# Twelve elementwise steps of a gated-recurrence and maxout kernel moved to GpSimd, with every engine's order kept

## The chip, the cores and the metric

One core of a Trainium2 chip runs the whole program. The metric is the device time of one execution in microseconds, the median of several runs. The engines are named as in the profile: PE (TensorE, the matrix unit), DVE (VectorE), ACT (ScalarE), POOL (GpSimd) and SP (SyncE, which issues most loads and stores). Each engine works through its own instructions in order; an instruction that waits for another engine or for a DMA holds up everything behind it on its own engine.

## What is computed

A gated linear recurrence over 4 batches, 8 heads, 768 steps and head size 48, with complex gates a, and then a feed-forward part whose hidden layer is the maximum of three products:

```python
mag = np.sqrt(a_re * a_re + a_im * a_im)
scale = np.minimum(mag, 0.999) / (mag + 1e-06)
a_re_n, a_im_n = (a_re * scale, a_im * scale)
...
for t in range(S):
    ar, ai = (a_re_n[:, :, t, :, None], a_im_n[:, :, t, :, None])
    new_re = ar * S_re - ai * S_im
    new_im = ar * S_im + ai * S_re
    kv = np.einsum('bhd,bhe->bhde', k[:, :, t], v[:, :, t])
    S_re, S_im = (new_re + kv, new_im)
    y[:, :, t] = np.einsum('bhd,bhde->bhe', q[:, :, t], S_re)
...
h = np.maximum(np.maximum(x @ w1, x @ w2), x @ w3)
return (h @ w_out).astype(np.float32)
```

x is y with the heads side by side: 3072 tokens of 384; w1, w2, w3 are 384 x 768, w_out is 768 x 384.

## The kernel before

**Tiling.** The tokens are cut into 12 groups (0 to 11) of two tiles, x and y, of 128 tokens each. For every group the program takes the gates to logarithm and angle (`gates`, `angles`), forms decay factors by matmuls with fixed 0/1 tables and exponentials, turns and scales k and q, transposes them, computes scores, states and outputs (`y`), and then the feed-forward part: `up` (three products and their maximum) and `op` (the product with w_out, for later groups by a seven-product scheme). The matmuls of group 0's feed-forward part begin while the weights are still being prepared.

**Order.** What runs when is written out by hand: SCHEDULE is a list of words, each `name:group`. `run` turns a word into instructions and the class `Bound` ties every instruction to the one before it on its engine, so each engine follows the list's order exactly. SLOTS hands out the banks of PSUM, and OTHER is a set of words that take the second of two engines where a step can run on either (VectorE for most).

**Weights.** They come in twelve blocks of 128 x 768 elements (0 to 11). For block i, `WLi` loads the raw words, `Wai` changes the type of their upper halves into a scratch (`ex`, the lower or the upper part of the tile `xhx`), and `Wei` (VectorE) merges the scratch with the lower halves into the weight tile. Blocks 0, 6, 10, 1, 4, 7 use the lower scratch, the others the upper one, so a `Wa` has to wait for the `We` before it on the same scratch. `Wgi` adds block i - i % 3 to block i, by an accumulating DMA that POOL issues, or on VectorE. `T`, `t` and `M` transpose blocks of w1 and multiply them with w_out; `Mn` reads the copies in vb2, vb3 and uk2, which `Z2`, `Z3` and `Z4` clear on POOL after that.

**Gates.** `sqr` and `sqi` square the two parts (tiles e and L), `add` sums them, `lnL` takes the logarithm, `expe` and `lne` make the correction of the 1e-06, `relu` writes the limited logarithm into the tile Ln, and `Lnop` adds the correction to it by an accumulating DMA from POOL. `abs`, `lnw`, `atan`, `turn` and others make the angle. `Cd` is a carry of a few numbers from one group to the next, two small DMAs from POOL for each tile, which `turn` of the next group waits for. `half` and `xor` work on sign bits.

**POOL before.** Besides those DMAs it makes the constant tables at the start, clears tiles, and in `CL` (`constants_late`) makes the late masks with the tile KB as scratch and clears the two score tiles atm0 and atm1.

Of the kernel before, what the change touches and what calls it, by code (L numbers as in the profile page):

```python
# [16 lines left out]
I32 = mybir.dt.int32  # L17
# [124 lines left out]
Px:10 P2:10 P6:10 P7:10  # L142
""".split())

ROOMS = {0: "w1", 3: "w2", 6: "wo", 11: "w1", 1: "w2", 9: "H", 10: "S", 2: "H", 4: "S", 5: "H", 7: "S", 8: "H"}
EX = (0, 6, 10, 1, 4, 7)

# [2 lines left out]
def kernel(  # L150
# [103 lines left out]

    def magnitude(out, in_):

        if other():
            dve.tensor_single_scalar(out=out.bitcast(I32), in_=in_.bitcast(I32), scalar=0x7FFFFFFF, op=OP.bitwise_and)
        else:
            activation(out=out, in_=in_, func=AF.Abs)  # L260
# [189 lines left out]
    def weight_step(i, step):  # L450

        dst, src = blocks[i]
        n, m = dst.shape[1:]
        ex = xhx[:, 0:KD] if i in EX else xhx[:, KD + KF:]
        ex = ex.rearrange("p f t -> p (f t)").rearrange("p (n m) -> p n m", n=n)
        if step == "a":
            high = T["raw", i].bitcast(BF).rearrange("p n (m w) -> p n m w", w=4)[:, :, :, 2]
            out = ex.bitcast(F16).rearrange("p n (m w) -> p n m w", w=2)[:, :, :, 1]
            if other():
                dve.tensor_single_scalar(out=out, in_=high, scalar=-1.0 if i in (0, 3, 6) else 1.0, op=OP.mult)  # L460
            else:
                activation(out=out, in_=high, func=AF.Copy, scale=-1.0 if i in (0, 3, 6) else 1.0)
        elif step == "e":
            low = T["raw", i].bitcast(I32).rearrange("p n (m w) -> p n m w", w=2)[:, :, :, 0]
            dve.scalar_tensor_tensor(out=dst.bitcast(I32), in0=low, scalar=13, in1=ex.bitcast(I32),
                                     op0=OP.logical_shift_right, op1=OP.bitwise_or)
        else:
            increase(dst, blocks[i - i % 3][0])
# [47 lines left out]
    def gates(g, cs, name):  # L516
# [19 lines left out]

        L, w, e, ar, ai = (part(nm) if (nm, g) in T else None for nm in ("L", "w", "e", "ar", "ai"))
        if name == "sqr":
            activation(out=e, in_=ar, func=AF.Square)
        elif name == "sqi":  # L540
            activation(out=L, in_=ai, func=AF.Square)
        elif name == "add":
# [5 lines left out]
        elif name == "expe":  # L548
            activation(out=e, in_=L, func=AF.Exp, scale=-0.5)
        elif name == "lne":  # L550
            if g >= ADDS and "relu:%d" % g not in OTHER:
                activation(out=e, in_=e, func=AF.Ln, scale=1e-6 * math.exp(-LNMAX), bias=math.exp(-LNMAX))
            else:
                activation(out=e, in_=e, func=AF.Ln, scale=1e-6, bias=1.0)
        elif name == "relu":
            T["Ln", g] = lns[g % 2]
            if other():
                dve.tensor_scalar(out=part("Ln"), in0=L, scalar1=-0.5, scalar2=-LNMAX, op0=OP.mult, op1=OP.max)
            else:
                activation(out=part("Ln") if g >= ADDS else L, in_=L, func=AF.Relu, scale=-0.5, bias=LNMAX)  # L560
# [26 lines left out]
        elif name == "xor":  # L587
            dve.scalar_tensor_tensor(out=ai.bitcast(I32), in0=ar.bitcast(I32), scalar=-0x80000000, in1=ai.bitcast(I32),
                                     op0=OP.bitwise_and, op1=OP.bitwise_xor)
        elif name == "half":  # L590
            dve.tensor_scalar(out=ar.bitcast(I32), in0=ar.bitcast(I32), scalar1=31, scalar2=HALF,
                              op0=OP.arith_shift_right, op1=OP.bitwise_and)
        elif name == "atan":
            activation(out=w, in_=w, func=AF.Arctan)
        elif name == "turn":
            dve.scalar_tensor_tensor(out=w, in0=w, scalar=-1.0 / math.pi, in1=ar, op0=OP.mult, op1=OP.add)
# [476 lines left out]
```

## Time and profile before

| | |
|---|---|
| three runs | 545.36, 543.21, 546.37 us; median 545.36 |
| the profiled execution | 543.15 us, its span 541.4 us |
| busy of the span | PE 95%, DVE 88%, ACT 68%, POOL 12% |
| granted TensorE clock | 1.00 |

A span is the time from the first instruction to the last. Times in the rows below are microseconds from its start. In a row of a timeline the first number is the start, the second the duration, then engine, line and operation, the tile written and the tiles read (buffer numbers left out), the form and the count; in square brackets the engine's idle time before it and what ended that. L210 is the line of the helper through which every instruction is recorded, so instructions are told apart by their tiles. A row of a group gives busy time and the mean of one in ns. Busy time of an engine says little by itself: what a step is worth depends on which engine ends last in its stage.

### The profile page before, as it was taken

What the parts mean: (1) busy time and instruction counts of PE and PEld (TensorE: products, weight loads), DVE (VectorE), ACT (ScalarE), POOL (GpSimd) and SP (SyncE); (2) the same over time, 40 slices, a digit from 0 to 9 for tenths busy, and PEclk for the clock granted to TensorE, in tenths of its full rate; (3) what the DMA queues carried; (4) which work ended last, traced back from release to release, by engine and by line L of the source; (5) the groups of instructions that cost most, each with busy time, mean ns of one, the idle gap of its engine ahead of it and who ended that gap; (6) DMA issues with size and microseconds to landing.
All of it is one profiled execution on the core that took longest, in us unless ns stands there. A gap on an engine that the chain in (4) does not pass through costs nothing.

```text
span 541.4 us, 24280 instructions
## 1 busy us (share of the span) xinstructions
PE 512.1 (95%) x10918; PEld 438.9 (81%) x10918; DVE 477.2 (88%) x746; ACT 367.9 (68%) x646; POOL 63.4 (12%) x107
## 2 busy tenths in 40 slices
PE   1499899999999999999999999999999999999996
PEld 1266778788988888888788888979888887988996
DVE  5999999999999999999789899899899979979414
ACT  7999887976874987667687576686779545451100
POOL 8424200110200110001200200020030020000000
PEclk9999999999999999999999999999999999999999
DMA  8999845553514045146226314035064042000001
GB/s 206 297 235 213 200 82 86 92 108 72 108 30 78 18 92 101 34 85 115 40 45 125 51 37 90 8 58 115 9 114 80 5 68 55 19 19 2 4 0 59
DMA packets 140152, 44.08 MB, mean 81 GB/s; under 512 B 130320, under 2 KB 138128, under 8 KB 140048
## 3 DMA queue, kind: packets, MB, share of 16 engines
q1 hardware_dynamic: 136272, 37.76, 32.9%
q0 software_dynamic: 3776, 4.76, 5.2%
q8 instruction: 86, 1.41, 1.1%
q14 instruction: 18, 0.15, 0.1%
HBM read 33.02 MB, written 4.72 MB: 70 GB/s over the span
## 4 chain that ended last, share of the span: by engine, by line
PE 86%; ACT 8%; DVE 2%; issue 2%; POOL 2%; DVEq 0%; ACTq 0%; POOLq 0%
PE up L210 35%; PE op L210 23%; PE y L210 7%; PE A L210 5%; PE tp L210 4%; PE dk L210 4%; PE sums L210 3%; PE cs L210 2%; PE F L210 2%; PE B L210 1%; ACT L L210 1%; ACT xhx L210 1%; ACT e L210 1%; ACT L210 1%; POOL cuts L210 1%
## 5 line engine op out<-in xcount | busy, mean ns | idle before, releaser
L210 PE MATMUL up<-xhx,w 128*128 128x256 f32 (+1 forms) x1062 | 177.7, 381 | 0.0
L210 PEld LDWEIGHTS up<-xhx,w 128*128 128x128 f32 (+1 forms) x1062 | 144.4, 163 | 24.8 <-issue 0.6
L210 ACT ACT_TABLE_LOAD x47 | 60.3, 1283 | 1.6 <-PEq L1057 0.8
L210 POOL DMA_DIRECT2D ar<-nf x40 | 33.3, 1226 | 153.8 <-DVE ar L210 102.5
L210 PE MATMUL op<-wo,xhx 128*128 128x192 f32 (+3 forms) x358 | 49.6, 368 | 0.0
L210 DVE TENSOR_TENSOR Q<-Q,f 112x512 f32<-112x512 f32 (+1 forms) x48 | 44.9, 953 | 0.0
L210 ACT COPY atm<-B 32x128 f32<-32x128 f32 x96 | 24.6, 256 | 28.9 <-PE B L210 16.7
L210 PE MATMUL y<-atm,vb 128*32 128x64 f32 x1152 | 39.8, 220 | 3.3 <-issue 3.3
L210 PE MATMUL y<-QG,g 112*32 112x64 f32 x1408 | 39.2, 219 | 1.4 <-issue 1.4
L210 PEld LDWEIGHTS op<-wo,xhx 128*32 128x32 f32 (+1 forms) x358 | 35.6, 149 | 4.3 <-issue 1.2
L210 PEld LDWEIGHTS y<-QG,g 112*32 112x32 f32 x1408 | 35.4, 109 | 4.1 <-issue 4.0
L210 PEld LDWEIGHTS y<-atm,vb 128*32 128x32 f32 x1152 | 34.7, 109 | 4.3 <-issue 2.5
L210 ACT ACTIVATE f<-F 48x232 f32<-48x232 f32 x96 | 34.2, 359 | 4.9 <-PE F L210 3.6
L210 DVE TENSOR_TENSOR xhx<-xhx,up 128x768 f32<-128x768 f32 x22 | 20.8, 951 | 18.2 <-PE up L210 18.1
L210 ACT ACTIVATE xhx<-up 128x768 f32<-128x768 f32 x17 | 13.8, 812 | 31.4 <-PE up L210 30.2
L210 PE MATMUL op<-wo,strassen 128*128 128x192 f32 (+1 forms) x272 | 33.0, 328 | 0.0
L210 PEld LDWEIGHTS A<-Q,K 112*32 112x32 f32 x1536 | 28.6, 110 | 5.0 <-issue 2.7
L210 DVE COPY_PREDICATED atm<-masko,A 128x256 f32<-128x256 uint8 x72 | 31.3, 438 | 1.4
L210 PE MATMUL A<-Q,K 112*32 112x80 f32 x1536 | 32.0, 233 | 0.7 <-issue 0.5
L210 PE MATMUL op<-w,strassen 128*128 128x192 f32 (+1 forms) x296 | 32.4, 328 | 0.0
L210 DVE TENSOR_TENSOR QG<-Q,f 112x1024 f32<-112x1024 f32 (+1 forms) x24 | 27.1, 1131 | 4.7 <-PE y L210 4.0
L210 PE MATMUL cs<-w,upto 128*32 128x192 f32 (+1 forms) x320 | 21.4, 344 | 9.4 <-POOL KB L210 6.7
(146 smaller groups left out, 1061.1 us busy)
## 6 DMA issues: line engine op xcount, KB each, us to landing
ai<-in_a_im_dram SPq DMA_DIRECT2D x24, 192.0 KB, 4.1
ar<-in_a_re_dram SPq DMA_DIRECT2D x24, 192.0 KB, 4.3
q<-in_q_dram SPq DMA_DIRECT2D x96, 48.0 KB, 2.9
k<-in_k_dram SPq DMA_DIRECT2D x96, 48.0 KB, 2.9
vb<-in_v_dram SPq DMA_DIRECT2D x96, 48.0 KB, 2.8
out_dram<-ot SPq DMA_DIRECT2D x23, 192.0 KB, 3.4
Ln<-e POOLq DMA_DIRECT2D x7, 384.0 KB, 4.9
w<-in_moe_w_dram SPq DMA_DIRECT2D x3, 767.2 KB, 7.9
```

The lines of the kernel that those rows point to most:

```text
L210: ins = f(*a, **kw)
```

## The change

A set POOLED of twelve words is added. Words in it run on POOL: the type changes Wa0, Wa6 and Wa11 (on VectorE before) and Wa3, Wa10, Wa9 and Wa1 (on ScalarE before); the limits relu:1 (VectorE) and relu:2, relu:4 (ScalarE); the squares sqr:2 and sqr:5 (ScalarE, by its Square function; on POOL a product of the tile with itself). A limit made on ScalarE leaves a constant factor that `lne` of its group takes out; for the moved ones `lne` uses the other form, as it did for limits on VectorE. The branches for `abs` and `half` are added too, but no word of theirs is in the set. SCHEDULE, SLOTS, OTHER and all else stay.

```diff
+POOLED = set("""
+Wa0:0 Wa6:0 Wa3:0 Wa10:0 Wa9:0 Wa1:0 Wa11:0 relu:1 relu:2 relu:4 sqr:2 sqr:5
+""".split())
...
     def magnitude(out, in_):
 
-        if other():
+        if T["word"] in POOLED:
+            pool.tensor_single_scalar(out=out.bitcast(I32), in_=in_.bitcast(I32), scalar=0x7FFFFFFF, op=OP.bitwise_and)
+        elif other():
...
-            if other():
+            if T["word"] in POOLED:
+                pool.tensor_single_scalar(out=out, in_=high, scalar=-1.0 if i in (0, 3, 6) else 1.0, op=OP.mult)
+            elif other():
                 dve.tensor_single_scalar(out=out, in_=high, scalar=-1.0 if i in (0, 3, 6) else 1.0, op=OP.mult)
...
         if name == "sqr":
-            activation(out=e, in_=ar, func=AF.Square)
+            if T["word"] in POOLED:
+                pool.tensor_tensor(out=e, in0=ar, in1=ar, op=OP.mult)
+            else:
+                activation(out=e, in_=ar, func=AF.Square)
...
-            if g >= ADDS and "relu:%d" % g not in OTHER:
+            if g >= ADDS and "relu:%d" % g not in OTHER | POOLED:
...
-            if other():
+            if T["word"] in POOLED:
+                pool.tensor_scalar(out=part("Ln"), in0=L, scalar1=-0.5, scalar2=-LNMAX, op0=OP.mult, op1=OP.max)
+            elif other():
                 dve.tensor_scalar(out=part("Ln"), in0=L, scalar1=-0.5, scalar2=-LNMAX, op0=OP.mult, op1=OP.max)
...
-            dve.tensor_scalar(out=ar.bitcast(I32), in0=ar.bitcast(I32), scalar1=31, scalar2=HALF,
-                              op0=OP.arith_shift_right, op1=OP.bitwise_and)
+            engine = pool if T["word"] in POOLED else dve
+            engine.tensor_scalar(out=ar.bitcast(I32), in0=ar.bitcast(I32), scalar1=31, scalar2=HALF,
+                                 op0=OP.arith_shift_right, op1=OP.bitwise_and)
```

What this does to the engines' lists is seen at three places. First POOL around CL, which is the block from the clearing of KB to the clearing of atm1. Before:

```order
L210 MEMSET g3_90 128x8x32
L210 MEMSET KB_100 128x384
L210 AFFINE_SELECT KB_100<-KB_100 128x128 x2
L210 COPY maskd_81<-KB_100 64x64 x2
L210 MEMSET KB_100 128x192
L210 AFFINE_SELECT KB_100<-KB_100 128x64 x6
L210 COPY masko_82<-KB_100 64x96 x2
L210 MEMSET atm0_91 128x512
L210 MEMSET atm1_92 128x512
```

And now, where the first two steps on `xhx_128` are Wa3 and Wa9 and the one at the end is Wa6:

```order
L214 MEMSET g3_90 128x8x32
L214 TENSOR_SCALAR xhx_128<-w2_126 128x768
L214 TENSOR_SCALAR xhx_128<-xhx_128 128x768
L214 MEMSET KB_100 128x384
L214 AFFINE_SELECT KB_100<-KB_100 128x128 x2
L214 COPY maskd_81<-KB_100 64x64 x2
L214 MEMSET KB_100 128x192
L214 AFFINE_SELECT KB_100<-KB_100 128x64 x6
L214 COPY masko_82<-KB_100 64x96 x2
L214 MEMSET atm0_91 128x512
L214 MEMSET atm1_92 128x512
L214 TENSOR_SCALAR xhx_128<-wo_127 128x768
```

Wa9 stands ahead of CL and Wa6 behind it. Next POOL from the clearing of vb2 (Z2) on, behind Wa11, relu:1 and Wa10; `ar<-nf` are the carries Cd, `Ln1<-e` is Lnop:1, `w1<-w0` and `w2<-w0` are accumulating DMAs Wg. Before:

```order
L210 MEMSET vb2_85 128x768
L210 DMA ar_210<-nf0_107 1x4x48 x2
L210 DMA Ln1_112<-e_267 128x768
L210 MEMSET vb3_86 128x768
L210 DMA ar_210<-nf1_108 1x4x48 x2
L210 MEMSET uk2_95 128x8x16
L210 DMA w1_125<-w0_124 128x3x256
L210 DMA w2_126<-w0_124 128x3x256
```

Now:

```order
L214 MEMSET vb2_85 128x768
L214 DMA ar_210<-nf0_107 1x4x48 x2
L214 TENSOR_SCALAR xhx_128<-w2_126 128x768
L214 DMA Ln1_112<-e_267 128x768
L214 TENSOR_TENSOR e_546<-ar_571 128x768
L214 MEMSET vb3_86 128x768
L214 DMA ar_210<-nf1_108 1x4x48 x2
L214 TENSOR_SCALAR Ln0_111<-L_544 128x768
L214 MEMSET uk2_95 128x8x16
L214 DMA w1_125<-w0_124 128x3x256
L214 DMA w2_126<-w0_124 128x3x256
```

Wa1 now stands ahead of Lnop:1, sqr:2 ahead of the second carry, and relu:2 ahead of the first Wg. Last VectorE around We6 (`w0<-wo,xhx`). Before:

```order
L210 TENSOR_SCALAR wo_127<-xhx_128 128x768
L210 TENSOR_SCALAR xhx_128<-wo_127 128x768
L210 TENSOR_TENSOR k0_101<-Ek0_113,k0_101 128x384
L210 TENSOR_SCALAR w0_124<-wo_127,xhx_128 128x3x256
L210 TENSOR_TENSOR uk0_93<-CS0_109,k0_101 128x8x2x48
```

Now:

```order
L214 TENSOR_SCALAR wo_127<-xhx_128 128x768
L214 TENSOR_TENSOR k0_101<-Ek0_113,k0_101 128x384
L214 TENSOR_SCALAR w0_124<-wo_127,xhx_128 128x3x256
L214 TENSOR_TENSOR uk0_93<-CS0_109,k0_101 128x8x2x48
```

The second row, Wa6, is gone from here; We6 reads what POOL writes. PE's and SP's lists are word for word as before, and ScalarE's has lost its eight steps and gained nothing.

## The prediction

> **What bounds the kernel now.** I read the page first (span, slices of busy time, the chain that ended last), then the busy time by stage, then the timelines of the stage that turned out to matter. The page:
>
> ```profile
> span 541.4 us, 24280 instructions
> PE   1499899999999999999999999999999999999996
> PE 86%; ACT 8%; DVE 2%; issue 2%; POOL 2%; DVEq 0%; ACTq 0%; POOLq 0%
> ```
>
> Of the last chain 86% is PE; the rest lies in the first slices, where PE is not yet full. The busy time by stage says where the border is (columns: window, length, then busy us and instructions of PE, PEld, DVE, ACT, POOL, granted clock, DMA share, GB/s):
>
> ```profile
> 20.00:50.00 30.00, 26.54 (x412) 18.09 (x414) 29.93 (x45) 29.78 (x50) 8.88 (x11) 1.00 0.97 248
> 50.00:62.00 12.00, 9.88 (x252) 8.03 (x252) 11.57 (x20) 11.92 (x24) 3.87 (x5) 1.00 1.05 197
> 62.00:100.00 38.00, 37.60 (x745) 30.89 (x748) 36.37 (x58) 31.07 (x53) 1.58 (x2) 1.00 0.49 96
> 100.00:300.00 200.00, 198.39 (x4130) 173.15 (x4119) 187.38 (x286) 151.14 (x259) 18.25 (x22) 1.00 0.41 78
> 300.00:530.00 230.00, 228.98 (x5296) 199.70 (x5295) 194.41 (x305) 127.30 (x231) 13.89 (x17) 1.00 0.22 42
> ```
>
> From 62 to 530 us PE idles 0.40 + 1.61 + 1.02 = 3.0 of 468 us at a granted clock of 1.00. The change touches no matmul, so this stretch neither shrinks nor swallows anything: it keeps whatever offset the first 62 us hand to it. From 20 to 50 us VectorE (29.93 of 30) and ScalarE (29.78) are both full and PE follows them; POOL has 21 us to spare. So the question is one number: when PE's `up` for group 0, which stands at 53.94 below, can start.
>
> **The change part by part: what it takes away.** VectorE loses Wa0, Wa6, Wa11 and relu:1, ScalarE loses Wa3, Wa9, Wa10, Wa1, relu:2, relu:4, sqr:2, sqr:5. The rows (start, duration), VectorE and then ScalarE:
>
> ```profile
> 10.84 0.68 DVE L210 TENSOR_SCALAR xhx<-w 128x768 f16<-128x768 bf16 x1 [1.38 <-POOL xhx L210]
> 19.07 1.02 DVE L210 SCALAR_TENSOR_TENSOR w<-w,xhx 128x768 int32<-128x768 int32 x1
> 24.80 0.61 DVE L210 TENSOR_SCALAR xhx<-wo 128x768 f16<-128x768 bf16 x1
> 25.75 0.96 DVE L210 SCALAR_TENSOR_TENSOR w<-wo,xhx 128x768 int32<-128x768 int32 x1
> 29.16 0.61 DVE L210 TENSOR_SCALAR xhx<-w 128x768 f16<-128x768 bf16 x1
> 29.65 0.55 DVE L210 TENSOR_SCALAR Ln<-L 128x768 f32<-128x768 f32 x1
> 30.11 0.96 DVE L210 TENSOR_TENSOR uk<-uk,En 128x768 f32<-128x768 f32 x1
> 49.06 0.95 DVE L210 SCALAR_TENSOR_TENSOR w<-w,ar 128x768 f32<-128x768 f32 x1
> ...
> 20.63 1.05 ACT L210 ACTIVATE xhx<-xhx 128x768 f16<-128x768 bf16 x1
> 45.91 0.83 ACT L210 ACTIVATE e<-ar 128x768 f32<-128x768 f32 x1
> 50.98 0.86 ACT L210 ACTIVATE L<-L 128x768 f32<-128x768 f32 x1
> ```
>
> VectorE: 0.68 + 0.61 + 0.61 + 0.55 = 2.45 us. ScalarE before 62 us: four type changes at 1.05, a limit and a square at about 0.85, 5.9 us. The limit relu:4 and the square sqr:5 fall after 62 us, where ScalarE fills 151 of 200 us beside a full PE: removed there they buy nothing, and POOL (18 of 200 us busy) has room for them: I cost them at nothing. If nothing new waited, the gain would be bounded by VectorE, the fuller engine that loses less: 2.45 us.
>
> **What a step costs on POOL.** No row of before shows such an operation there. The nearest:
>
> ```profile
> L210 POOL COPY mid<-mid 64x64 f32<-64x64 f32 x1 | 0.2, 232 | 0.1
> L210 POOL COPY cuts<-cuts 64x29 f32<-64x29 f32 x1 | 0.2, 202 | 0.1
> 40.47 0.74 POOL L210 MEMSET vb<- 128x768 f32 x1 [3.02 <-PE wm L210]
> ```
>
> Two copies give (232 - 202) / 35 = 0.86 ns an element over a fixed part, so 202 + 739 x 0.86 = 0.84 us for 768 elements. Lower end 0.74 (a bare write of that size), upper end 1.7 (twice the copy, as for two reads). I take 1.1 for a type change (the strided halves cost ScalarE 1.05 where a plain pass costs 0.86, a quarter more), 0.95 for a limit (nearest the copy) and 1.6 for a square (two reads, nearest the upper end).
>
> **What it adds: a queue.** POOL works in order, and its own rows stand in the way:
>
> ```profile
> 12.22 0.41 POOL L210 MEMSET KB<- 128x384 f32 x1
> 19.33 0.98 POOL L210 MEMSET atm<- 128x512 f32 x2
> 35.95 1.50 POOL L210 DMA_DIRECT2D Ln<-e  x1
> 41.27 1.62 POOL L210 DMA_DIRECT2D ar<-nf  x2
> 46.83 2.62 POOL L210 DMA_DIRECT2D w<-w  x2 [0.35 <-issue]
> ```
>
> The first two are the ends of CL, the late masks: 12.22 to 20.31, 8.1 us without a gap. Before, it ran while POOL had nothing else. Now Wa9 stands ahead of it and Wa6 behind it, and Wa9 has to wait. It overwrites the scratch that We3 (VectorE, 19.07 to 20.09) reads, and it needs its weight block:
>
> ```profile
> 14.24 0.58 SPq L210 DMA_DIRECT2D xhx<-in_moe_w_out_dram  x1
> DMA to landing us min/median/max: 4.5/5.9/7.4
> ```
>
> issued at 14.24, so landed between 18.7 and 20.6 (the four loads into this tile took 4.5 to 7.4, and ScalarE read the block at 20.63 without waiting). VectorE is up to 0.7 us earlier by then, since Wa0's slot is gone. So, step by step, by the values above:
>
> 1. Wa9 starts at 20.1 and ends at 21.2; CL 8.1 us to 29.3; Wa6 to 30.4. VectorE's We6 stood at 25.75 and waits until 30.4: 4.65 late. Queued behind it on VectorE are uk, QG, QB: everything. Wa11 and relu:1 are gone from its list (29.16 to 30.11, 0.95 us), so from there VectorE is 30.4 - 25.75 - 0.95 = 3.7 late. ScalarE, whose abs:1 now waits for relu:1 on POOL and its copies for PE, follows.
> 2. Behind Wa11, relu:1 and Wa10 comes the clearing of vb2, which must wait for the product M0, and M0 for uk:
>
> ```profile
> 28.16 1.10 PE L210 MATMUL tp<-ident,uk 64*112 64x64 f32 x16
> 36.31 4.04 PE L210 MATMUL wm<-wo,vb 128*128 128x384 f32 x12
> ```
>
> (the second row is M1, alike and without a wait inside). uk ends at about 32.3, transposes 33.4, M0 37.4, clearing 38.2, two carry DMAs (1.6 us of issue) 39.8, Wa1 40.9. Only then does POOL issue Lnop:1, at 40.9 for 35.95. We1 on VectorE (3.7 late, about 41.9) finds Wa1 just done.
> 3. sqr:2 overwrites the tile that Lnop:1 reads. ScalarE used to wait for that; now POOL does, with the carry Cdy:0 behind it. Landing times (operation, count, KB each, us from issue to landing):
>
> ```profile
> Ln<-e POOLq DMA_DIRECT2D x1, 384.0 KB, 8.5
> ar<-nf POOLq DMA_DIRECT2D x2, 0.8 KB, 4.7
> w<-w POOLq DMA_DIRECT2D x1, 384.0 KB, 4.9
> ```
>
> Lnop:1 took 8.5 while the loads filled the DMA engines; a block of that size took 4.9 elsewhere. 40.9 + 4.9 to 8.5 (I take 6.7) = 47.6; sqr:2 to 49.2, clearing 49.9, the second carry issued near 50.7, landed 55.4. turn:1 on VectorE (49.06 before, 52.8 if 3.7 late) waits for it: 6.3 late.
> 4. relu:2 needs ScalarE's logarithm of the group, 50.98 to 51.84 before, 55.5 if 3.7 late; relu:2 ends at 56.5. Behind it on POOL stands, after a 0.2 us clearing, the accumulating DMA Wg1, which completes the weight block that `up` reads. It left at 46.83; now it cannot leave before 56.7, and lands 4.9 later (its own row above) at 61.6.
>
> ```profile
> 53.94 1.60 PE L210 MATMUL up<-ot,w 128*128 128x128 f32 x12
> 60.23 2.16 issue
> ```
>
> `up` thus starts at 61.6 instead of 53.94: **7.7 us late**. The path over turn:1 gives 6.3 and lies inside that. Behind it PE has its whole remaining list, so the end moves by the same 7.7.
>
> **The sum.** The rows are of one execution, 543.15 us with a span of 541.4, 1.75 around it. 543.15 + 7.7 = 550.9. The median of the three runs is 545.36 (543.21 to 546.37), 2.2 above that execution; with the same 7.7 it is 553.1. I forecast **553 us**. What is uncertain in the 7.7: prices of a step from 0.74 to 1.7 in Wa9, Wa6 and relu:2 (-0.9 to +2.0), Wa9's start (-0.6 to +0.5), and PE's stall of 2.16 at 60.23, which nothing in the trace explains and which may not recur (-2.2 to 0). Own range of this case: +4 to +10, 549.5 to 555.5.
>
> **Rival: the shared port (slower still).** VectorE's two-input steps beside POOL's work:
>
> ```profile
> 12.70 1.21 POOL L210 TENSOR_SCALAR_AFFINE_SELECT KB<-KB 128x128 f32<-128x128 f32 x2
> 13.10 0.56 DVE L210 TENSOR_TENSOR ai<-ai,L 128x384 f32<-128x384 f32 x1 [0.25 <-ACT L L210]
> 13.57 0.68 DVE L210 TENSOR_TENSOR w<-w,e 128x384 f32<-128x384 f32 x1
> ```
>
> Two alike steps of 384 elements took 0.56 and 0.68 beside two short selects; if each of POOL's longer steps held VectorE off for its own time, the type changes and limits that run beside a full VectorE (Wa0 and Wa3 ahead of Wa9; Wa11, relu:1, Wa10 after We6; Wa1) would add up to 6 us, of which perhaps 4 reach `up`, since VectorE waits anyway around Wa6 and sqr:2: 553.1 + 4 = 557. Against it: 0.12 us is all that two selects of 1.21 us cost here. The Trainium skill (SBUF - State Buffer, "Who interferes with whom") says that a VectorE instruction with two SBUF inputs and a GpSimd instruction that reads SBUF exclude each other for the whole instruction; by it this is the likely course, and the 0.12 us here neither proves nor excludes it.
>
> **Rival: only the last queue counts.** If ScalarE and VectorE, shorter by 5.9 and 2.45 us, made good all the delay of We6, relu:2 would still wait for the logarithm's end at 51.84, and Wg1 would leave at 51.84 + 0.95 + 0.2 = 53.0, land at 57.9 and hold `up` by 4.0; without the stall of 2.16, by 1.8. Time 547 to 549. For it: ScalarE loses most and was full. Against it: the delay sits in VectorE, which loses little.
>
> **Rival on the other side: faster.** The steps leave two full engines for one that is 70% idle, and 2.45 us come off: 542.9. It decides at We6: Wa6 must be done by 25.75, so Wa9 must start by 25.75 - 1.1 - 8.1 - 1.1 = 15.4. Its block cannot land before 18.7, and We3 stands at 19.07. I see no way round that in an order that is kept. That the change does less than it says holds only for the branch of `half`, whose words are not in POOLED.
>
> **How the numbers follow.** Forecast 0.57, port 0.22, last queue only 0.13, faster 0.08. About 0.5% (2.7 us) is what a measurement of this kernel can tell from no change. Faster by more: 0.05 (most of the last case); within: 0.03 of that case and 0.04 of the last-queue case, 0.07; slower: 0.88. The range leaves out the faster case and the far ends: 547 to 560.
>
> **What would show it.** Right: VectorE idle some 4 to 5 us ahead of We6 with POOL named as releaser; CL's rows running from about 21 to 29; POOL idle ahead of sqr:2 until a DMA lands; `up` of group 0 starting near 61 to 62; from there the same stage lengths as before. Wrong: We6 near 25 with CL before Wa9's end; a POOL step far off 0.7 to 1.7 us; VectorE's two-input rows longer by a microsecond beside POOL's (then the port); or `up` late by 8 and the end not.

## The result and the profile after

The change makes the kernel slower, 2.5 times as much as forecast:

| | median us | runs | ratio to before, 95% interval |
|---|---|---|---|
| before | 545.87 | 4 (543.21 to 547.09) | |
| the change | 565.56 | 4 (565.18 to 566.37) | 1.0394, 1.0357 to 1.043 |
| forecast | 553.0 (547 to 560) | | |

That is 19.7 us where 7.7 were forecast. The page of the profiled execution of the change (565.7 us): the span, the busy tenths of PE, POOL and PE's granted clock in 40 slices, and the last chain by engine.

```profile
span 563.9 us, 24284 instructions
...
PE   1458679999999999999989999999999999999996
...
POOL 8697530002312011000120020020020020000000
PEclk9979979999999999999999999999999999999999
...
PE 78%; DVE 8%; POOL 4%; DMA 3%; issue 3%; ACT 2%; SPq 1%; DVEq 0%; POOLq 0%
```

PE is full from the seventh slice on and was from the sixth. In the last chain VectorE has 8% where it had 2%, POOL 4% for 2%, and DMAs 3% where they had none. The busy time by stage (columns as before: window, length, busy us of PE, PEld, DVE, ACT, POOL, granted clock, DMA share, GB/s):

```profile
20.00:50.00 30.00, 20.84 (x234) 13.53 (x230) 20.86 (x26) 19.80 (x31) 26.38 (x26) 0.89 0.72 190
50.00:62.00 12.00, 9.42 (x208) 6.17 (x197) 11.23 (x17) 7.89 (x16) 4.06 (x5) 0.86 0.57 125
100.00:300.00 200.00, 195.99 (x4222) 169.86 (x4219) 186.77 (x286) 149.54 (x258) 22.67 (x23) 1.00 0.39 72
```

From 20 to 50 us VectorE and ScalarE, 29.9 and 29.8 busy before, are down to 20.86 and 19.80, and POOL is up from 8.88 to 26.38: the bound of this stretch has moved to POOL. Between 100 and 300 PE works 195.99 of 200, 2.4 less than before (198.39): stalls put down to "issue", to which the runs below come back. POOL's timeline (start, duration, idle before it and its releaser in brackets) reads, in this order: Wa0 and Wa3, Wa9, the first and last clearing of CL, Wa6, Wa11, relu:1, Wa10, the clearing of vb2, Wa1, Lnop:1, sqr:2, relu:2, and the accumulating DMAs Wg.

```profile
10.53 2.42 POOL L214 TENSOR_SCALAR xhx<-w 128x768 f16<-128x768 bf16 x1
14.16 2.68 POOL L214 TENSOR_SCALAR xhx<-w 128x768 f16<-128x768 bf16 x1 [0.24 <-DVE ar L214]
21.33 3.04 POOL L214 TENSOR_SCALAR xhx<-xhx 128x768 f16<-128x768 bf16 x1 [4.48 <-DVE w L214]
24.28 0.42 POOL L214 MEMSET KB<- 128x384 f32 x1
30.00 0.98 POOL L214 MEMSET atm<- 128x512 f32 x2
31.07 2.38 POOL L214 TENSOR_SCALAR xhx<-wo 128x768 f16<-128x768 bf16 x1
33.39 2.38 POOL L214 TENSOR_SCALAR xhx<-w 128x768 f16<-128x768 bf16 x1
35.70 2.86 POOL L214 TENSOR_SCALAR Ln<-L 128x768 f32<-128x768 f32 x1
38.53 2.82 POOL L214 TENSOR_SCALAR xhx<-strassen 128x768 f16<-128x768 bf16 x1
42.81 0.74 POOL L214 MEMSET vb<- 128x768 f32 x1 [1.45 <-PE wm L214]
44.82 4.64 POOL L214 TENSOR_SCALAR xhx<-w 128x768 f16<-128x768 bf16 x1
49.38 0.94 POOL L214 DMA_DIRECT2D Ln<-e  x1
53.43 1.49 POOL L214 TENSOR_TENSOR e<-ar 128x768 f32<-128x768 f32 x1 [3.11 <-DMA Ln<-e]
64.11 3.51 POOL L214 TENSOR_SCALAR Ln<-L 128x768 f32<-128x768 f32 x1 [6.94 <-ACT L L214]
67.73 3.97 POOL L214 DMA_DIRECT2D w<-w  x3
```

The order is the one the prediction walked through, and so is each wait: CL stands behind Wa9, the clearing behind M0, sqr:2 behind the landing of Lnop:1, Wg behind relu:2. What is off is the length: type changes of 2.4 to 4.6 us for 1.1, limits of 2.9 and 3.5 for 0.95; the square, 1.49, was taken at 1.6. The same points on VectorE and PE (We6; QG; turn:1; then M0 and the first `up` of group 0):

```profile
33.49 1.57 DVE L214 SCALAR_TENSOR_TENSOR w<-wo,xhx 128x768 int32<-128x768 int32 x1 [6.64 <-POOL xhx L214]
35.85 1.30 DVE L214 TENSOR_TENSOR QG<-Q,f 112x512 f32<-112x512 f32 x1
61.42 0.96 DVE L214 SCALAR_TENSOR_TENSOR w<-w,ar 128x768 f32<-128x768 f32 x1
```

```profile
37.11 5.58 PE L214 MATMUL wm<-wo,vb 128*128 128x384 f32 x12
73.11 2.90 PE L214 MATMUL up<-ot,w 128*128 128x128 f32 x12 [6.72 <-DMA w<-w]
```

We6 waits 6.64 us for Wa6, as forecast by place, and then takes 1.57 where it took 0.96; QG takes 1.30 for 0.69; M0 takes 5.58 us where the prediction reckoned with 4.04. That turn:1 is reached by way of the second carry is seen in the chain that ended last (start, duration): POOL issues it, it lands at 61.30, and turn:1 starts, though VectorE had itself only just finished the step before.

```profile
55.60 0.51 POOL ar L214
56.11 5.19 DMA ar<-nf
...
61.42 0.06 DVE w L214
```

`up` starts at 73.11: 19.2 us behind its 53.94. The medians are 19.7 apart, so most of the delay is handed on to the end, as forecast. Not exactly, though: the spans of these two profiled executions are 22.5 apart (541.4 and 563.9), so in this pair another 3.3 us were lost behind the start of `up`, 1.3 of them in `up` itself (2.90 for 1.60). How much of that belongs to the kernel and how much to the single execution, one profile of each can't tell.

### The profile page after: what moved, and what is told of

Read it like the earlier page. It is cut to its first block, busy times and chain, and to the rows that moved or that the text cites. A ratio compares the mean times of both kernels' runs of the same rounds, so it can differ in the third digit from the quotient of the medians.

```text
span 563.9 us, 24284 instructions
## 1 busy us (share of the span) xinstructions
PE 516.1 (92%) x10918; PEld 442.7 (79%) x10918; DVE 480.9 (85%) x742; ACT 362.6 (64%) x638; POOL 93.7 (17%) x119
## 4 chain that ended last, share of the span: by engine, by line
PE 78%; DVE 8%; POOL 4%; DMA 3%; issue 3%; ACT 2%; SPq 1%; DVEq 0%; POOLq 0%
PE up L214 31%; PE op L214 21%; PE y L214 6%; PE A L214 4%; PE tp L214 4%; PE dk L214 4%; PE sums L214 2%; PE cs L214 2%; DVE w L214 2%; POOL xhx L214 2%; PE F L214 1%; PE B L214 1%; SPq L214 1%; PE wm L214 1%; DMA w<-w 1%
```

## The experiments

Ratios are to the kernel before on the same chip, with 95% intervals; "up" is the start of the first `up` in the profile of that run (53.94 before, 73.11 in the change). Where a diff shows only the table POOLED, the rest is the change. One caution for all profiles: the change and its near twin without the late pair share every step up to the border, yet their `up` stands at 73.11 and 71.39. Differences under some 2 us between two profiles prove nothing by themselves.

**One queue undone at a time.** The first three kernels each remove one place where POOL's order makes somebody wait, the fourth puts one step of the change into the kernel before, and the fifth undoes two places at once.

```diff
-Wa0:0 Wa6:0 Wa3:0 Wa10:0 Wa9:0 Wa1:0 Wa11:0 relu:1 relu:2 relu:4 sqr:2 sqr:5
+Wa0:0 Wa6:0 Wa3:0 Wa10:0 Wa9:0 Wa1:0 Wa11:0 relu:1 relu:4 sqr:2 sqr:5
```

> The changed kernel with the limit of group 2 alone put back on ScalarE. Theory (queue on POOL, steps of 2.4 to 4.6 us as the trace of the changed kernel shows): the first accumulating DMA of the weights leaves near 59 us instead of 67.7 and lands near 64.5, so the first matmul of up stands behind the sums and starts near 66.5 to 67.5 instead of 73.1. Time 565.6 - 6 = 559 to 560. Rival (shared port and the lower granted clock hold PE back, not this queue): up moves by less than 2 us, time 564 to 566.

```diff
-Wa0:0 Wa6:0 Wa3:0 Wa10:0 Wa9:0 Wa1:0 Wa11:0 relu:1 relu:2 relu:4 sqr:2 sqr:5
+Wa0:0 Wa6:0 Wa3:0 Wa10:0 Wa1:0 Wa11:0 relu:1 relu:2 relu:4 sqr:2 sqr:5
```

> The changed kernel with the type change of block 9 alone put back on ScalarE, so that nothing on POOL ahead of the late masks waits for VectorE. Theory (queue): the masks run from about 17 to 24 us instead of 24.3 to 31, the merge of block 6 on VectorE starts near 27 instead of 33.5, all of POOL's later steps come 6 to 7 us earlier, up starts near 67; time 559 to 560. Rival (the delay is the sum of long steps and port conflicts, whatever their order): the gain is about one step, 3 us; time 562 to 563.

```diff
-mulw1:0 mulai1:0 stt1:0 atan0:0 turn0:0 Wa3:0 half1:0 Liy:1 Lqx:0 Lix:1 sqi:1 sqr:1 csx:0 atan1:0 mqx:0 We3:0 xor:1
-tx:0 WL9:0 Wa9:0 nfx:0 afx:0 sbx:0 sax:0 turn1:0 csy:0 f1x:0 f2x:0 add:1 uqx:0 tpqx:0 WL6:0 CL:0 Ekx:0 We9:0 Wa6:0
+mulw1:0 mulai1:0 stt1:0 atan0:0 turn0:0 Wa3:0 CL:0 half1:0 Liy:1 Lqx:0 Lix:1 sqi:1 sqr:1 csx:0 atan1:0 mqx:0 We3:0 xor:1
+tx:0 WL9:0 Wa9:0 nfx:0 afx:0 sbx:0 sax:0 turn1:0 csy:0 f1x:0 f2x:0 add:1 uqx:0 tpqx:0 WL6:0 Ekx:0 We9:0 Wa6:0
```

> The changed kernel with the late masks moved in the written order from behind the type change of block 9 to ahead of it (behind that of block 3); the same twelve steps on POOL, the same amount of work. Theory (queue): POOL's 4.5 us of waiting ahead of that type change are filled by the masks, everything behind comes 4 to 4.5 us earlier; the merge of block 6 starts near 29, up near 69, time 561 to 562. Rival (amount of work and port): no change, 565 to 566.

Measured: relu:2 back 1.0242 (1.0189 to 1.0296), `up` at 65.13; Wa9 back 1.0298 (1.0252 to 1.0345), `up` at 66.79; CL first 1.0327 (1.0268 to 1.0387), `up` at 69.08. The third removes no POOL step, and its `up` is 4.0 earlier for the order alone; its interval still overlaps the change's. We6 follows Wa6 in each: it starts at 28.80 with Wa9 back, where the expectation had 27, and at 29.47 with CL first. At `up` all three go the way of the queue theory, the first by more than expected. The times say so less clearly: with Wa9 back the ratio is the rival's (its 562 to 563 us are a ratio of about 1.03), and with CL first it lies between theory and rival.

And the kernel before with one step of the change alone (POOLED and the branches that it steers as in the change):

```diff
+POOLED = set("""
+relu:2
+""".split())
```

> The kernel before with relu:2 alone on POOL. Theory (last queue, with the price now measured): the logarithm of group 2 ends at 51.8 as before, the limit takes 2.9 to 3.5, a clearing 0.2, so Wg1 leaves near 55.3 instead of 46.8, lands some 5 later, and up starts near 60.3 instead of 53.94: 6.4 later, time 6 above before, ratio 1.011 to 1.013. By the price that the prediction took (0.95) it would be 4 later, less the stall of PE that is there in before at 60 us: ratio 1.003 to 1.007. Rival that one step hides in the slack of POOL: within 1 us of before.

Measured 1.0125 (1.007 to 1.018), Wg leaving at 55.48 and `up` at 60.80: by the measured price, not by the one the prediction took. Alone, this one step costs a third of the whole loss.

```diff
-Wa0:0 Wa6:0 Wa3:0 Wa10:0 Wa9:0 Wa1:0 Wa11:0 relu:1 relu:2 relu:4 sqr:2 sqr:5
+Wa0:0 Wa6:0 Wa3:0 Wa10:0 Wa1:0 Wa11:0 relu:1 relu:4 sqr:2 sqr:5
```

> The change without relu:2 and Wa9 on POOL (ten steps left). Theory (one queue, whose parts add up): the gains of the two kernels that undid one of them, 8 and 6 us, add up: ratio 1.0394 less 0.0258 is about 1.013, up near 60. Rival (another wait, sqr:2 behind the landing of Lnop:1 with the second carry behind it, or VectorE slowed by the other POOL steps, holds up by itself): ratio 1.018 to 1.024, up near 63 to 65.

Measured 1.0147 (1.0089 to 1.0206), `up` at 61.8: the gains add up, 0.0152 and 0.0096 alone and 0.0247 together.

**What a step costs on POOL.** Behind the last output block of the kernel before stand single steps on 128x768, first with VectorE idle, then beside it.

```diff
     program(SCHEDULE, 0)
+    for r in range(2):
+        pool.tensor_scalar(out=l0, in0=x0, scalar1=-0.5, scalar2=-LNMAX, op0=OP.mult, op1=OP.max)
+        pool.tensor_single_scalar(out=l0, in_=x0, scalar=-0.5, op=OP.mult)
+        pool.tensor_copy(out=l0, in_=x0)
+        pool.tensor_tensor(out=l0, in0=x0, in1=x0, op=OP.mult)
+        pool.tensor_single_scalar(out=half, in_=high, scalar=1.0, op=OP.mult)
+        pool.tensor_copy(out=half, in_=high)
+        pool.memset(l0, 0.0)
+    for kind in ("scalar", "tensor", "memset", "one"):
...
```

> The kernel before, and behind its last output block a row of single steps on 128x768 elements whose results nobody reads: first, with VectorE idle, on POOL a limit (two operations), a product with a constant, a copy, a square, a type change with the strides of Wa, the same as a copy, a clearing, all twice; then four stretches of twelve VectorE steps, of which the last eight run beside four POOL steps. Theory price (the step itself is slow on POOL): with VectorE idle a limit takes 2.5 to 3, a type change 2.2 to 2.6, a square about 1.5, a clearing 0.74. Rival (the steps were slow only because VectorE and the DMAs ran beside them): with VectorE idle all take 0.8 to 1.2, as two short copies of the kernel before would give. On the shared port: if a two-input VectorE step and a POOL step shut each other out, a VectorE step of 0.95 becomes 3 to 4 beside a POOL limit, and a POOL limit is not stretched by more than one VectorE step each; if they share piece by piece, a VectorE step is some 0.3 to 0.7 longer and a POOL step half as long again; beside a clearing nothing changes. The stretch behind the border is that of the kernel before, so its stalls of PE inside the products y are those of the kernel before: none between 150 and 250 us, if the late pair makes them.

POOL's timeline at that place, VectorE idle (the first row holds two steps, the limit with 2.79 us and the product with a constant with 2.14):

```profile
541.23 5.01 POOL L210 TENSOR_SCALAR Ln<-ot 128x768 f32<-128x768 f32 x2 [100.08 <-DVE ot L210]
546.31 0.82 POOL L210 COPY Ln<-ot 128x768 f32<-128x768 f32 x1
547.22 1.47 POOL L210 TENSOR_TENSOR Ln<-ot 128x768 f32<-128x768 f32 x1
548.66 2.36 POOL L210 TENSOR_SCALAR Ln<-xhx 128x768 f16<-128x768 bf16 x1
551.09 1.04 POOL L210 CAST Ln<-xhx 128x768 f16<-128x768 bf16 x1
552.03 0.75 POOL L210 MEMSET Ln<- 128x768 f32 x1
```

The price theory holds, the contention rival falls: with nothing beside it, a limit takes 2.79 us and a type change made as a product 2.36. The copy rows of before gave 0.84 for 768 elements, and a copy does take 0.82; the mistake was to price a product with a constant by a copy. VectorE beside POOL (three two-input steps alone and eight beside POOL's four, which are one square and three limits, then four squares, then one square and three clearings; in the last row VectorE's eight steps have one input, beside one square and three limits):

```profile
565.41 2.94 DVE L210 TENSOR_TENSOR CS<-CS 128x768 f32<-128x768 f32 x3
568.28 10.05 DVE L210 TENSOR_TENSOR strassen<-CS 128x768 f32<-128x768 f32 x8
584.85 12.48 DVE L210 TENSOR_TENSOR strassen<-CS 128x768 f32<-128x768 f32 x8
601.09 9.05 DVE L210 TENSOR_TENSOR strassen<-CS 128x768 f32<-128x768 f32 x8
612.31 7.34 DVE L210 TENSOR_SCALAR strassen<-CS 128x768 f32<-128x768 f32 x8
```

Alone a step takes 2.94 / 3 = 0.98, so eight take 7.84. Four squares add 4.64, 1.16 each. One square and three clearings add 1.21, which is the square: clearings cost these two-input steps nothing. One square and the part of three limits that fell beside the eight add 2.2, far less than the nearly 10 us for which those POOL steps ran: the two engines don't shut each other out for a whole step. The one-input steps pay too: 0.58 each alone, they take 7.34 for 4.67. POOL's steps also get longer, a square 2.06 for 1.47 and a limit 3.4 for 2.79.

The same code up to the tail shows PE 48.34 busy of 50 between 150 and 200 us, like the change (47.87) and unlike the first profile of before (50.00): PE's stalls of 1 to 2 us there can come in one execution of this code and be missing in another, without the late pair.

**Cheaper forms, and the price as forecast.**

```diff
-            if T["word"] in POOLED:
-                pool.tensor_single_scalar(out=out, in_=high, scalar=-1.0 if i in (0, 3, 6) else 1.0, op=OP.mult)
+            if T["word"] in POOLED and i not in (0, 3, 6):
+                pool.tensor_copy(out=out, in_=high)
+            elif T["word"] in POOLED:
+                pool.tensor_single_scalar(out=out, in_=high, scalar=-1.0, op=OP.mult)
```

> The change with the four type changes that need no sign (Wa9, Wa10, Wa1, Wa11) made on POOL as a copy between types, 1.04 alone, and not as a product with 1.0, 2.36 alone; the same numbers come out. Theory (the price of the form is what was mis-sized): Wa9 1.3 to 2.0 shorter, so We6 and all behind it that much earlier; Wa1 3 shorter, so Lnop:1, sqr:2 and the second carry another 3 earlier; up 4 to 6 earlier than in the change, ratio 1.028 to 1.033. Rival (POOL is slow beside a full VectorE whatever the form): these steps take 2 and more there too, and the ratio stays above 1.036.

```diff
-                pool.tensor_single_scalar(out=out, in_=high, scalar=-1.0 if i in (0, 3, 6) else 1.0, op=OP.mult)
+                pool.tensor_copy(out=out, in_=high)
...
-                pool.tensor_scalar(out=part("Ln"), in0=L, scalar1=-0.5, scalar2=-LNMAX, op0=OP.mult, op1=OP.max)
+                pool.tensor_copy(out=part("Ln"), in_=L)
```

> The change with every POOL step at about the price that the prediction took: all seven type changes as copies between types (1.04 alone; Wa0, Wa3 and Wa6 without their sign) and the three limits as plain copies (0.82 alone; without factor and limit), the squares as they are. The output is not the reference's: signs and limits are left out. Theory (the queue of the prediction was right and only the prices were wrong): up starts at 61 to 63 as forecast (61.6), ratio 1.012 to 1.019. Rival (there is more to it than the price of a step, such as the shared port): up at 65 or later, ratio 1.022 or more.

Copies for four type changes gave 1.0336 (1.0303 to 1.0369), `up` at 71.6: a time between the two expectations, and at `up` 1.5 earlier where 4 to 6 were expected, a miss. With everything at about the forecast price it was 1.0272 (1.0243 to 1.0301) and `up` at 69.0 instead of 61.6: my theory that only the price was wrong fell. We6 starts at 30.64 there, where the prediction said 30.4; what goes wrong comes behind it. VectorE's We6, uk and QG, and later the product beside Wa1, in that kernel:

```profile
30.64 1.68 DVE L214 SCALAR_TENSOR_TENSOR w<-wo,xhx 128x768 int32<-128x768 int32 x1 [4.04 <-POOL xhx L214]
32.24 1.57 DVE L214 TENSOR_TENSOR uk<-CS,k 128x768 f32<-128x768 f32 x1
33.73 1.49 DVE L214 TENSOR_TENSOR QG<-Q,f 112x512 f32<-112x512 f32 x1
43.86 2.15 DVE L214 TENSOR_TENSOR ai<-ai,L 128x768 f32<-128x768 f32 x1 [1.28 <-ACT L L214]
```

These four took 0.96, 0.96, 0.69 and 0.95 before: 3.3 us lost beside POOL's steps, and 1.28 of waiting for ScalarE. POOL's steps didn't keep their price either: its copies took 1.05 to 2.28 and sqr:2 took 3.03.

**Without reads.** Two kernels keep the queue and take the reads away.

The first has, for a type change as for limits and squares:

```diff
-                pool.tensor_single_scalar(out=out, in_=high, scalar=-1.0 if i in (0, 3, 6) else 1.0, op=OP.mult)
+                pool.tensor_copy(out=out[:, :, 0:8], in_=high[:, :, 0:8])
+                pool.memset(out, 0.0)
```

> The change with each of the twelve POOL steps made a copy of a few columns (which keeps its waits) and a clearing of the whole tile: some 0.8 to 1.0, the price that the prediction took, and no reads to speak of, so no loss on VectorE (beside clearings it lost nothing in the run of prices). The output is not the reference's: the values of the type changes, limits and squares are left out. Four kernels then stand as a square: the change (dear, reads), the one priced as forecast with copies (cheap, reads, up at 69.0, ratio 1.027), this one (cheap, no reads) and the next (dear, no reads). Theory (port and price both count, and PE's slow clock after its wait for uk is the rest): up at 62 to 65.5, ratio 1.014 to 1.021. Rival (reads on POOL do not matter, all of the rest is PE's clock): up at 68 to 69, ratio 1.025 to 1.029.

The second clears three times for a type change, four times for a limit, twice for a square:

```diff
-                pool.memset(out, 0.0)
+                for r in range(3):
+                    pool.memset(out, 0.0)
```

> As the one with short clearings, but each step as long as the change's steps were with VectorE idle: the few columns and three clearings for a type change (some 2.3), four for a limit (3.0), two for a square (1.5). The output is not the reference's, the same values are left out. Theory (port and price both count): VectorE keeps its durations and POOL's Wa1 is not stretched to 4.6, so up is 2.5 to 5 earlier than in the change's 73.1, 68 to 70.5, ratio 1.029 to 1.035. Rival (the price alone): as the change, up 72 to 73.5, ratio 1.037 to 1.042.

The short one: 1.0232 (1.0196 to 1.0268), `up` at 65.72: outside both ranges, the time halfway between them and `up` next to the theory's. By time it can't be told from the 1.0272 with reads, since the intervals overlap; by `up` it is 3.3 earlier, and VectorE's rows say why (an earlier step, then We6, uk and QG):

```profile
11.82 1.04 DVE L214 TENSOR_SCALAR ar<-ar 128x384 int32<-128x384 int32 x1
...
29.91 0.96 DVE L214 SCALAR_TENSOR_TENSOR w<-wo,xhx 128x768 int32<-128x768 int32 x1 [4.20 <-POOL xhx L214]
30.79 0.95 DVE L214 TENSOR_TENSOR uk<-CS,k 128x768 f32<-128x768 f32 x1
31.66 0.68 DVE L214 TENSOR_TENSOR QG<-Q,f 112x512 f32<-112x512 f32 x1
```

None of the last three is longer than before. But clearings aren't free for every step: the first row, a step with one input, took 1.04 beside clearings for 0.50 before, and 1.09 in the kernel with long ones. The long one missed both theories: 1.0462 (1.0423 to 1.0502), `up` at 76.2. A clearing of the strided half took 0.98, not 0.74, so a type change took 3.2 there for the 2.4 to 3.0 of the change, and the few columns ahead of Wa1's clearings alone took 2.91. It is no fair pair to the change; all it shows is that a longer queue with hardly any reads is enough for such a loss.

**Reads without a queue.**

```diff
             constants_late()
+            flat = spare.rearrange("p a n -> p (a n)")
+            pool.memset(flat, 1.0)
+            for r in range(10):
+                pool.tensor_scalar(out=flat, in0=flat, scalar1=-0.5, scalar2=-LNMAX, op0=OP.mult, op1=OP.max)
```

> The kernel before with ten POOL steps behind CL, in the stretch from 20.3 to 34 where POOL does nothing: a limit over 320 elements of a tile that nobody else uses, in place, 1.0 to 1.4 each. Nobody waits for them. Theory (port): VectorE's steps beside them get about a quarter longer, as in the run of prices, 2 to 3.5 us in all, VectorE is the fuller engine there, and up and the end move by 1.5 to 3.5 us: ratio 1.003 to 1.006. Rival (POOL's work costs only those who wait for it): ratio 0.998 to 1.001.

Measured 1.0127 (1.0093 to 1.0161), `up` at 59.35: more than twice what the theory expected, and the rows show the step of it that failed (POOL's ten steps):

```profile
20.27 22.88 POOL L210 TENSOR_SCALAR spare<-spare 128x320 f32<-128x320 f32 x10
43.09 0.73 POOL L210 MEMSET vb<- 128x768 f32 x1
```

```profile
22.61 1.21 DVE L210 TENSOR_TENSOR uq<-CS,q 128x768 f32<-128x768 f32 x1
28.41 0.93 DVE L210 TENSOR_TENSOR QB<-Q,f 112x512 f32<-112x512 f32 x1
```

VectorE pays 0.25 per step (0.95 to 1.21, 0.69 to 0.93), some 2.0 in all, the low end of what was expected. POOL pays more: 2.29 a step beside a full VectorE, where 1.0 to 1.4 was expected. So the ten steps, meant to end by 34, ended at 43.1 and became a queue after all: the clearing of vb2, at 34.07 before, and the DMAs behind it came 9 us late.

**PE's clock.**

```diff
-            for n, mat in enumerate((mid, rest)):
+            for n, mat in [(0, mid), (1, rest)] * (5 if x == 1 else 1):
```

> The change, with PE given something to do while it waits for uk: the 16 small products of the second half's sums are made five times over, the same values into the same bank, some 6 us from 28 to 35 where PE stood idle in the change. Theory (PE's granted clock falls after an idle stretch and M0 pays for it): the granted clock from 35 to 40 is above 0.9 instead of 0.50, M0 takes 4.0 to 4.8 instead of 5.6 to 6.7 and ends 1 to 2 earlier, the clearing of vb2 and all of POOL's queue behind it too: up 0.5 to 2 earlier, ratio 1.035 to 1.039. Rival (M0 is longer for another reason, its weight loads or a shared path): M0 stays at 5.6 or more, ratio 1.039 to 1.043, since ScalarE waits some us for the last sums.

The windows from 35 to 40 us, first of the change, then of this kernel (the third figure from the end is the granted clock):

```profile
35.00:40.00 5.00, 3.93 (x21) 2.62 (x22) 5.00 (x7) 1.40 (x2) 5.00 (x3) 0.50 0.70 132
```

```profile
35.00:40.00 5.00, 5.00 (x38) 3.14 (x36) 4.85 (x7) 2.00 (x3) 5.00 (x3) 1.00 0.63 122
```

```profile
35.06 4.14 PE L214 MATMUL wm<-wo,vb 128*128 128x384 f32 x12
```

M0 took 4.14 us at a clock of 1.00, instead of 5.58 at 0.50: the idle stretch ahead of it, 6.6 us in the change and 2.9 here, is the cause. `up` came at 70.8, 2.3 earlier, but most of that is not the clock's gain: We6 already started 1.6 earlier here (31.86 for 33.49), since Wa9 did. The time missed both: 1.0714 (1.0664 to 1.0765). Behind the border PE worked 190.94 of the 200 us from 100 to 300 for the change's 195.99, with its stalls put down to "issue". These 64 added products, long done by then, are the only change to PE's list. Why this kernel stalls more later stays open; the verdict on the clock rests on the rows of M0 alone.

**Behind the border.**

The kernel before with the late pair alone, the change without it, and the kernel before with all late steps:

```diff
+POOLED = set("""
+relu:4 sqr:5
+""".split())
```

> Before, with only the limit of group 4 and the square of group 5 on POOL: the two steps that lie in the stretch in which PE is full. Theory (queue): POOL has room there and nobody waits, the time is that of before within 1 us. Rival (every POOL step takes port time from a VectorE that is 90% busy): 1 to 3 us more than before.

```diff
-Wa0:0 Wa6:0 Wa3:0 Wa10:0 Wa9:0 Wa1:0 Wa11:0 relu:1 relu:2 relu:4 sqr:2 sqr:5
+Wa0:0 Wa6:0 Wa3:0 Wa10:0 Wa9:0 Wa1:0 Wa11:0 relu:1 relu:2 sqr:2
```

> The change without relu:4 and sqr:5, which lie behind the border. Theory (as forecast, they cost nothing): the time of the change, ratio near 1.039. Rival (the late pair brings the stalls of PE inside the products y between 150 and 250 us that all five kernels with it show and the kernel before does not): the stall of 1.4 to 1.9 us there is gone and the ratio is near 1.035.

```diff
+POOLED = set("""
+relu:4 relu:5 relu:6 relu:7 relu:8 relu:9 relu:10 relu:11 sqr:5 sqr:6 sqr:7 sqr:8 sqr:9 sqr:10 sqr:11
+""".split())
```

> The kernel before with all limits and squares that lie behind the border made on POOL: the limits of groups 4 to 11 and the squares of groups 5 to 11, fifteen steps in place of the pair. Theory (behind the border PE is full, VectorE and ScalarE have slack, so a late step on POOL costs nothing, and the 0.4% of the pair was spread between runs): ratio 0.999 to 1.005. Rival (each late step costs about 1 us, as the 2.1 us of the pair would say): ratio 1.02 to 1.03.

The pair alone: 1.004 (1.001 to 1.0069), 2.1 us, as the rival said. The change without it: 1.034 (1.0285 to 1.0396), its interval overlapping the change's own; the time is the rival's, and the stall is gone, with PE busy all of the 100 us from 150 to 250. Fifteen late steps: 1.0083 (1.0057 to 1.0109), between the two expectations, some 4.5 us or 0.3 each. So a late step isn't free, and the pair costs something between 0.6 (two of the fifteen) and 2 us; the runs don't settle it closer. Whether it does so by those stalls stays open too. All thirteen profiles with the pair lose 1.4 us or more of PE between 150 and 250; of the six without it, four lose nothing, but two (the single steps behind the last block, and three copies, below) lose 1.7 and 1.9.

**Better orders.**

The kernel with four copies, and in its table of the order:

```diff
-tx:0 WL9:0 Wa9:0 nfx:0 afx:0 sbx:0 sax:0 turn1:0 csy:0 f1x:0 f2x:0 add:1 uqx:0 tpqx:0 WL6:0 CL:0 Ekx:0 We9:0 Wa6:0
+tx:0 WL9:0 CL:0 Wa9:0 nfx:0 afx:0 sbx:0 sax:0 turn1:0 csy:0 f1x:0 f2x:0 add:1 uqx:0 tpqx:0 WL6:0 Ekx:0 We9:0 Wa6:0
...
-g0y:0 WL5:0 Wa5:0 relu:2 ty:1 nfy:1 sumsy:1 Eqy:1 Eky:1 g1y:0 expw:2 KBy:0 g2y:0 QBy:0 Z4:0 g3y:0 Wg1:0 U01x:0 u01x:0
-Wg2:0 abs:2 addw:2 Eny:1 sumsx:1 Ekx:1 Lvy:0 dky:0 h1y:0 By:0 b0y:0 half:2 QGy:0 We5:0 U02x:0 h2y:0 Wg5:0 Wg4:0 b1y:0
+g0y:0 WL5:0 Wa5:0 ty:1 nfy:1 sumsy:1 Eqy:1 Eky:1 g1y:0 expw:2 KBy:0 g2y:0 QBy:0 Z4:0 g3y:0 Wg1:0 U01x:0 u01x:0
+Wg2:0 relu:2 abs:2 addw:2 Eny:1 sumsx:1 Ekx:1 Lvy:0 dky:0 h1y:0 By:0 b0y:0 half:2 QGy:0 We5:0 U02x:0 h2y:0 Wg5:0 Wg4:0 b1y:0
```

> All twelve steps still on POOL, the four type changes without a sign as copies, and the order of POOL not kept: the late masks CL ahead of Wa9, and relu:2 behind the two accumulating DMAs Wg1 and Wg2. Theory (the loss is made by queues on POOL and the price of a step): the gains of casts (about 0.010), CL first (0.007) and relu:2 out of the way (0.015) add up, ratio 1.005 to 1.012, up near 58 to 60, held then by the carry behind Lnop:1 and sqr:2 or by VectorE. Rival (moving twelve steps to POOL costs by itself, by VectorE's steps getting longer): ratio 1.016 or more.

The same copies and CL ahead of Wa9 as just shown, relu:2 where it was, and three steps on POOL:

```diff
-Wa0:0 Wa6:0 Wa3:0 Wa10:0 Wa9:0 Wa1:0 Wa11:0 relu:1 relu:2 relu:4 sqr:2 sqr:5
+Wa9:0 Wa10:0 Wa11:0
```

> The kernel before with CL ahead of Wa9 and only Wa9, Wa10 and Wa11 on POOL, as copies between types, where POOL has nothing to do and no DMA behind them waits. Theory (ScalarE loses 2.1 and VectorE 0.6 of work, and VectorE pays some 0.3 to 0.6 for each POOL step beside it): between 0.996 and 1.002. It would beat the kernel before only if ScalarE set the pace from 20 to 50 us. Rival (CL waits for Wa3 or Wa9 for CL, and We9 or We11 is late): 1.004 to 1.01.

All twelve steps on POOL in a better order and partly as copies: 1.0131 (1.0104 to 1.0158), `up` at 60.2, a little more than the theory's range and less than the rival's. Two thirds of the loss go without taking a step back; the rest stays. Three copies where POOL is idle: 1.0002 (0.9977 to 1.0027), no better than before. One of them, Wa11, took 4.19 us beside the full VectorE, for 1.04 alone:

```profile
25.59 4.19 POOL L214 CAST xhx<-w 128x768 f16<-128x768 bf16 x1 [3.91 <-DVE xhx L214]
```

None of these kernels beats the kernel before.

## Why the prediction was right in kind and wrong in size

The steps, point by point. The column "near the forecast price" is the kernel with short clearings, whose steps lasted 1.1 to 2.3 us with their few columns and read next to nothing.

| point, us | before | forecast | the change | near the forecast price, hardly any reads |
|---|---|---|---|---|
| We6 starts (step 1) | 25.75 | 30.4 | 33.49 | 29.91 |
| M0 ends (step 2) | 33.9 | 37.4 | 42.7 | 39.6 |
| Lnop:1 leaves (step 2) | 35.95 | 40.9 | 49.38 | 43.81 |
| turn:1 starts (step 3) | 49.06 | 55.4 | 61.42 | 54.86 |
| relu:2 starts (step 4) | 53.75 on ScalarE | 55.5 | 64.11 | 57.17 |
| Wg leaves (step 4) | 46.83 | 56.7 | 67.73 | 59.36 |
| `up` starts | 53.94 | 61.6 | 73.11 | 65.72 |

Right: each of the four waits, its place, who is queued behind whom, that `up` waits for Wg last, that the stretch behind the border hands most of the delay on, and the sign. The three kernels that undo one wait each show it at `up`, and two of the gains add up. One wait was not foreseen: We1, said to find Wa1 "just done", waited 2.32 us for it.

Wrong: 11.5 us of the 19.2. Between the profiles of three kernels the gap at `up` splits into three terms. Each is a difference of two single profiles, so good to some 2 us only; the rows named with each show that it exists, not its exact size.

1. **The price of a step, 4.1 us** (73.11 less the 69.0 of the kernel with copies). This is the step "I take 1.1 for a type change, 0.95 for a limit", with an upper bound of 1.7. A type change measured 2.36 and a limit 2.79 alone, outside the bounds. The nearest rows were copies, a different form. The square, taken at 1.6, took 1.49. The stated uncertainty, prices "in Wa9, Wa6 and relu:2", also left out Wa1, which stands on the path and took 4.64.
2. **Reads on POOL, 3.3 us** (69.0 less 65.72; shown on VectorE's rows, not by the time; it holds what both engines lose, VectorE's steps and POOL's own). The prediction had it as the rival of the shared port and sized it at 4 on top of 553. It is no rival to the queue but adds to it: VectorE is delayed by the queue and slowed by the reads. The evidence held against it, 0.12 us beside two selects, came from short selects on 128 elements and said nothing about 768. In the change it bites even before We6: the prediction had VectorE "up to 0.7 us earlier" at We3, and We3 started 1.2 later (20.29 for 19.07): three of VectorE's steps beside Wa0 and Wa3 took 1.24, 1.92 and 1.20 for 0.54, 0.50 and 0.68.
3. **PE's clock and the rest, 4.1 us** (65.72 less 61.6). Step 2 costed M0 by a row of M1 "without a wait inside", 4.04 us. But the same step made PE wait for uk, and after such a wait M0 took 5.1 to 6.7. In the kernel with short clearings M0 alone is 2.65 longer; ScalarE's copy of the transposes behind it, then VectorE's product, come late, and relu:2 starts 1.7 later than forecast (57.17 for 55.5), though We6 started 0.5 earlier. By these figures the clock's part is about 2 of the 4.1, an estimate. The remainder is relu:2 in two instructions (57.17 to 59.27), 1.1 more than taken, and Wg landing 6.4 after leaving, where 4.9 was taken. In the change a second product, M2, was slowed as well after an idle stretch, 5.83 for 4.14 (granted clock 0.72 from 52 to 58 us), and ScalarE, which makes the logarithm that relu:2 waits for, stood 2.16 us behind it.

The Trainium skill (TensorE: Matmul & The Clock Gate, "Part 1: The HAM clock gate") says that an idle window of about 3.4 us halves PE's clock until it has been busy for about as long; the 0.50 here and its cure by keeping PE busy agree. The prediction had found the wait and not asked what it does to the clock.

The rule cited in the prediction (the Trainium skill, SBUF - State Buffer, "Who interferes with whom") has the losing engine shut out for the whole instruction, and clearings left out of it. For two-input steps the clearings agree: 0 us. The whole instruction does not: beside relu:1, which took 2.86, QG lost 0.61 (1.30 for 0.69), and beside ten steps that took 2.29 each it lost 0.25 each.

"Only the last queue counts" fell, since We6 and VectorE stayed late to the end. "Faster" fell with Wa9, which started at 21.33, not by 15.4. The late pair, costed at nothing because PE is full there, costs something between 0.6 and 2 us. The stall of 2.16 at 60.23 did not recur at its place in the change; others came later.

## What to carry to other kernels

Work given to an idle engine is paid for by whatever already stands in that engine's queue: walk down its list and ask of each step what it waits for and who waits behind it, and move the steps behind the DMAs that others need. Price each step by a row of the same operation and form, and when there is none, put a probe of that form in a quiet stretch first; a copy says nothing about a product with a constant. Where a forecast makes an engine wait, re-price what that engine does next, and where two engines run side by side, let both get longer.

## What the runs showed of the hardware

- On POOL, with VectorE idle and 128x768 f32, a copy took 0.82 us, a product of two tensors 1.47, a product with one constant 2.14 and a limit (two operations with constants) 2.79.
- Where a two-input step of VectorE lost time beside a POOL step, it lost 0.25 beside 320 elements read and mostly 0.6 to 1.2 beside 768, less than the POOL step's own length; beside clearings it lost nothing. Beside Wa9, Wa1 and relu:2 of the change it lost at most 0.2, and these three were themselves stretched, to 3.04, 4.64 and 3.51. A one-input step, 0.50 before, took 1.04 and 1.09 beside clearings.
- POOL can suffer more than VectorE. Wa1, 2.36 alone, took 4.64 beside a full VectorE; a copy of 1.04 took 4.19; a few columns took 2.91. How POOL's turn is decided stays open.
- A kernel with sixty-four more matmuls at 28 us had more PE stalls hundreds of us later, 9 of 200 us idle where the change had 4; nothing here shows why.
